# States' gate and val in seven products: one edit at the end of a recurrent-attention and SwiGLU kernel on one Trainium2 core

## The chip, the cores and the metric

The kernel runs on one core of a Trainium2 chip. TensorE (PE) multiplies, VectorE (DVE) and ScalarE (ACT) work element by element, GpSimd (POOL) does some more of that, and SyncE (SP) issues most of the DMA transfers. The engines run beside each other and wait for each other by semaphores; each takes its own instructions in the order in which the program lists them. The metric is the device time in microseconds; lower is better. All data are float32.

## The reference

Two stages follow each other. The first is a cross attention between 512 tokens and 32 states for each of 8 batches and 8 heads of width 64. The second is a SwiGLU feed-forward layer on all 8 x (512 + 32) = 4352 rows.

```python
# attention, per batch and head: x is (512, 64), state is (32, 64)
xread = softmax(scale * x @ state.T) @ state      # 512 rows: the tokens
sread = softmax(scale * state @ x.T) @ x          # 32 rows: the states
rows  = concatenate([xread, sread])               # heads side by side: 512 columns

# feed-forward, d_model = 512, d_ff = 1536
xn  = rows / sqrt(mean(rows**2) + 1e-6) * rms_g
g   = xn @ w_gate
val = xn @ w_val
out = (g * sigmoid(g) * val) @ w_out
```

What the change touches is `g`, `val` and the output of the 8 x 32 = 256 state rows.

## The kernel before

**Seven products.** A product of two matrices, each cut into 2 x 2 blocks, takes eight products of blocks. By the Strassen-Winograd scheme it takes seven, at the price of sums and differences of blocks. The kernel uses it for the output of every row but batch 0's (`project_seven`) and for gate and val of the tokens of batches 1 to 7 (`hidden_seven`). In `hidden_seven` a pair of hidden blocks (`mp`, six pairs of 2 x 128 columns) is one round: seven products, accumulated in the PSUM banks x, y and z, copied by ScalarE (`copies`, L570), added by VectorE (`sums`, L584). Bank x is written four times in a round: after its first and second product ScalarE copies it, after its third VectorE adds it to `c22`, and after that the round's last product is accumulated on top. Between the third and the last stand the first two products of the next pair.

**Stages.** Up to about 126 us the weights are brought into their form and batch 0 is computed. Then one period of about 98 us follows for each of batches 1 to 7: gate, val and output of one batch's tokens, and between them the attention of the next batch. After batch 7 comes the stretch of the states, which this case is about.

**The states before.** All 256 state rows are held transposed in `xsT` (4 parts of 128 model columns x 256 rows). For each of the 12 hidden blocks, `hidden` (L475) computes gate and val by plain products, 4 calls each over the 4 parts, with weights from `w_m` (L832). Here the stationary operand is a 128 x 128 block of weights and the moving operand has 256 columns. ScalarE applies Silu (L492), VectorE multiplies (L496), and for the upper six blocks it forms the sums that the output needs (L501, L503). Then `project_seven(NT, store_states)` gives the output, with the order of its steps written out in L839: p a product, c a copy by ScalarE, k a sum by VectorE. Each of its seven products is 6 calls (L677) of 256 columns. Its stores are cut into four pieces of 32 rows each, one DMA per piece, all on SyncE (L746).

**Order.** Inside `tc.manual_schedule` the order of TensorE, VectorE and ScalarE is dealt by hand: each letter of `ORDER` (up to batch 0) and `PERIOD` (each later batch) takes one step of the generator of that name. In the last period the stream `a` runs `state_norm` (L404): it squares `xsT` (L407), sums over the model columns (L412), takes the power -1/2 on GpSimd (L245), spreads the result over the rows by two transposes (L252) and scales `xsT` (L422). `paced` (L769) lets six letters pass after each of its steps. The stretch of the states stands behind the last period, with no order by hand.

**Weights in transit.** The weights of one pair, gate and val together, are one tile `w_m` of 1 MB, fetched from `w_d` by SyncE (`fetch`, L140) into one of three buffers. A buffer is fetched into again when TensorE has used it. When the stretch of the states begins, the tiles of pairs 0 to 2 are there; those of pairs 3 to 5 are fetched during it.

Of the kernel before, what the change touches and what calls it, by code (L numbers as in the profile page):

```python
# [17 lines left out]
P = 128  # L18
# [14 lines left out]
    "aaksacccassppakckpaaackasaapakapaskaaaswpksksswsxxwxxpxcspcskx"  # L33
)
# [3 lines left out]
def kernel(  # L38
# [365 lines left out]
    def state_norm():  # L404

        sq = one.tile([P, NI, NT], F32, name="sqT", tag="eS")
        SE.activation(out=sq, in_=xsT, func=ACTF.Square, scale=DM ** -0.5)  # L407
        yield
        sp = aps.tile([P, NT // P], F32, name="at")
        for r in range(NT // P):  # L410
            for i in range(NI):
                TE.matmul(out=sp[:, r:r + 1], lhsT=sq[:, i, P * r:P * r + P], rhs=ones,  # L412
                          start=(i == 0), stop=(i == NI - 1))
# [61 lines left out]
    def hidden(m, n, lhs, rhs, banks):  # L475


        gp, vp = [], []
        t = []
        h = hb[:, m, :]  # L480

        def products():
            for k, to in enumerate((gp, vp)):
                to.append(banks[k].tile([P, S], F32, name="pv" if banks[k] is vps else "f"))
                for i, r in enumerate(rhs):
                    TE.matmul(out=to[0][:, 0:n], lhsT=lhs(i, k), rhs=r,  # L486
                              start=(i == 0), stop=(i == len(rhs) - 1))
                yield

        def silu():  # L490
            t.append(two.tile([P, S], F32, name="t", tag="g"))
            SE.activation(out=t[0][:, 0:n], in_=gp[0][:, 0:n], func=ACTF.Silu)  # L492
            yield

        def gated():
            VE.tensor_tensor(out=h[:, 0:n], in0=t[0][:, 0:n], in1=vp[0][:, 0:n], op=ALU.mult)  # L496
            if "s" in seven and m >= HM:

                k = m - HM
                upper, lower = hb[:, k, 0:n // 2], hb[:, k, n // 2:n]  # L500
                VE.tensor_tensor(out=seven["s"][:, k, 0:n // 2], in0=lower, in1=hb[:, m, n // 2:n],  # L501
                                 op=ALU.add)
                VE.tensor_tensor(out=lower, in0=upper, in1=lower, op=ALU.subtract)  # L503
            yield

        return products(), silu(), gated()


# [11 lines left out]
    def hidden_seven(b):  # L520


        pairs = [{} for mp in range(NM // 2)]

        def product(ps, lhs, rhs, start):
            for i in range(2):
                TE.matmul(out=ps[:, i, :], lhsT=lhs[:, i, :], rhs=rhs, start=(start and i == 0),  # L527
                          stop=True, skip_group_check=True)

        def products():  # L530
            tt = aT_t[b]
            b11, t3, b21, b22 = (aT_s[b][:, e, HS * i:HS * i + HS]
                                 for e in range(2) for i in range(2))

            def first(mp, q):
                v, _ = v_sb[b, mp]
                a11, q["a12"], q["s3"], q["a22"] = (v[:, e, :, k, :]
                                                    for k in range(2) for e in range(2))
# [4 lines left out]
                _, vs = v_sb.pop((b, mp))  # L543
                q["vs"] = vs
                product(q["z"], vs[:, 0], tt[:, 0], True)
                yield

            def last(q):
                product(q["x"], q["a22"], tt[:, 2], False)

            yield from first(0, pairs[0])
            for mp, q in enumerate(pairs):
                if mp:
                    last(pairs[mp - 1])
                    yield
                product(q["x"], q["vs"][:, 1], tt[:, 1], False)
                yield
                product(q["z"], q["vs"][:, 2], b22, False)
# [9 lines left out]
            yield  # L568

        def copies():  # L570
            for mp, q in enumerate(pairs):
                g = q["g"] = two.tile([P, 2, 2, HS], F32, name="g", tag="g")
                SE.copy(g[:, :, 0, :], q["x"])
                yield
                q["c"] = seven["c22"].tile([P, 2, HS], F32, name="c22")
                SE.copy(q["c"], q["z"])
                yield
                SE.copy(g[:, :, 1, :], q["x"])  # L578
                yield
                SE.activation(out=hb[:, 2 * mp:2 * mp + 2, :], func=ACTF.Tanh, scale=0.5,  # L580
                              in_=g.rearrange("p m c t -> p m (c t)"))
                yield

        def sums():  # L584
            for mp, q in enumerate(pairs):
                h = hb[:, 2 * mp:2 * mp + 2, :]
                g = q["g"]
                for to, ps in ((g[:, :, 1, :], "z"), (g[:, :, 0, :], "y"), (q["c"], "x")):
                    VE.tensor_tensor(out=to, in0=to, in1=q[ps], op=ALU.add)  # L589
                    yield  # L590
                VE.scalar_tensor_tensor(out=h, in0=h, scalar=1.0, op0=ALU.add, op1=ALU.mult,  # L591
                                        in1=g.rearrange("p m c t -> p m (c t)"))
                yield
                for i, val in ((1, q["c"]), (0, q["x"])):
                    half = h[:, :, HS * i:HS * i + HS]
                    VE.scalar_tensor_tensor(out=half, in0=half, scalar=0.5, in1=val,
                                            op0=ALU.mult, op1=ALU.mult)
                    yield
                if 2 * mp >= HM:
                    k = 2 * mp - HM  # L600
                    upper, lower = (hb[:, k:k + 2, HS * i:HS * i + HS] for i in range(2))
                    VE.tensor_tensor(out=seven["s"][:, k:k + 2, :], in0=lower, in1=h[:, :, HS:S],
                                     op=ALU.add)
# [57 lines left out]
    def project_seven(n, store):  # L661
# [7 lines left out]
        def product(name, lhs, rhs):  # L669
# [5 lines left out]
            for r in range(R):  # L675
                for k in range(HM):
# [28 lines left out]
        def copies():  # L705

            for what, name in (("p1", "x"), ("p5", "z"), ("u2", "x"), ("c21", "x")):
                for r in range(R):
                    to = kept[what, r] = pool.tile([P, HD], F32, name="ot2")
                    SE.copy(to, banks[name][:, r, :])  # L710
                    if what == "c21":
                        store(R + r, 0, HD, to)
# [30 lines left out]
    def store_states(r, c0, n, ot):  # L743
        for j in range(4):
            r0 = T * (4 * r + j) + S
            nc.sync.dma_start(out=out[r0:r0 + Ns, c0:c0 + n], in_=ot[Ns * j:Ns * j + Ns, :])  # L746
# [3 lines left out]
    def of_batch_0(part):  # L750

        for m in range(NM):
            if m not in parts_0:
                parts_0[m] = hidden(m, S, lambda e, k, m=m: v_sb[0, m // 2][0][:, e, m % 2, k, :],
                                    [aT_s[0][:, e, :] for e in range(2)], (vps, vps))
# [50 lines left out]
    for b in range(1, B):  # L806
# [3 lines left out]
        h, t, u = hidden_seven(b)  # L810
# [10 lines left out]
        else:  # L821
            others = paced(state_norm())
# [48 lines left out]
```

## Time and profile before

| | us |
|---|---|
| median of 3 runs (806.21 to 806.81) | 806.23 |
| the profiled execution | 806.07 |
| its span, first to last instruction | 804.3 |
| from the states' gate and val to their output (742.17 to 781.02) | 38.85 |
| the states' output (781.02 to 800.05) | 19.03 |
| the tail behind the last matmul | 4.25 |

The page cuts the span into 40 slices and shows the busy tenths of each engine in them:

```profile
PE   4599999999999999999999999999999999999997
PEld 2243444788778887888778877888788877888886
DVE  4999996588347842786368834784278626841121
ACT  4888864553245323543255324532354325401110
POOL 0000003530154005500443025400550044200000
PEclk9699999999999999999999999999999999999999
```

Each digit is a fortieth of the span, some 20 us. PEld is TensorE's loading of stationary operands, which can lie beside its matmuls. The periods are seen as a pattern of about five digits in DVE, ACT and POOL; in the last three digits (from about 744 us) these engines have little to do. PEclk is the clock granted to TensorE, in tenths of full speed.

A row of the tables below names the line, the engine, the operation, what is written from what, the shape, the count, the busy time in us, the mean in ns of one, and the idle time before it. In a timeline the first column is the start and the second the time from there to the end of the last instruction of that row.

### The profile page before, as it was taken

Reading aid. Unit: us, or ns where it says so; the run is one execution under the profiler, and the core shown is the slowest. Engines: PE = TensorE matmul, PEld = TensorE weight load, DVE = VectorE, ACT = ScalarE, POOL = GpSimd, SP = SyncE. Lnnn points to the kernel's source line nnn. Section 1 sums busy time; section 2 is a strip of 40 time slices with the busy share of each in tenths; the row PEclk is TensorE's granted clock in tenths of the full one; section 3 lists DMA queues with packets and bytes.
Section 4 is the critical chain, followed back from the end, with each engine's and each line's share of the span. In section 5 each row is a group of like instructions: output and inputs, shape, how many; then the busy total and the mean of one; then the engine's idle time right before and its main releaser. Section 6 shows DMA issues by size and latency. Waiting matters only on the chain.

```text
span 804.3 us, 11772 instructions
## 1 busy us (share of the span) xinstructions
PE 779.2 (97%) x4678; PEld 592.5 (74%) x4678; DVE 493.3 (61%) x746; ACT 341.1 (42%) x560; POOL 178.4 (22%) x215
## 2 busy tenths in 40 slices
PE   4599999999999999999999999999999999999997
PEld 2243444788778887888778877888788877888886
DVE  4999996588347842786368834784278626841121
ACT  4888864553245323543255324532354325401110
POOL 0000003530154005500443025400550044200000
PEclk9699999999999999999999999999999999999999
DMA  9788745600172007300460017200630035001401
GB/s 294 229 287 298 262 160 185 259 31 13 36 269 105 1 24 248 152 1 18 150 241 17 14 44 261 106 1 20 233 115 2 13 145 208 2 14 38 147 12 27
DMA packets 61591, 94.09 MB, mean 117 GB/s; under 512 B 38752, under 2 KB 46432, under 8 KB 54624
## 3 DMA queue, kind: packets, MB, share of 16 engines
q1 hardware_dynamic: 59456, 92.81, 33.4%
q8 instruction: 37, 0.61, 0.3%
q10 hardware_dynamic: 2080, 0.52, 0.3%
q14 instruction: 18, 0.15, 0.1%
HBM read 78.12 MB, written 15.20 MB: 116 GB/s over the span
## 4 chain that ended last, share of the span: by engine, by line
PE 94%; DVE 4%; issue 0%; ACT 0%; DMA 0%; SPq 0%; DVEq 0%
PE f L677 35%; PE f L527 32%; PE f L486 5%; PE f L617 5%; PE pv L486 4%; PE at L444 3%; PE pv L444 3%; PE at L273 2%; PE at L282 1%; PE at L327 1%; PE at L341 1%; PE at L388 1%; DVE ex L223 1%; PE at L376 1%; DVE raw L219 1%; PE at L252 1%
## 5 line engine op out<-in xcount | busy, mean ns | idle before, releaser
L677 PE MATMUL f<-wo,hb 128*128 128x256 f32 x540 | 124.1, 382 | 0.6 <-ACT ot L710 0.5
L527 PE MATMUL f<-aT_s,v 128*128 128x256 f32 x504 | 119.6, 381 | 0.0
L677 PEld LDWEIGHTS f<-wo,hb 128*128 128x128 f32 x540 | 101.4, 190 | 20.5 <-ACT ot L710 7.3
L527 PEld LDWEIGHTS f<-aT_s,v 128*128 128x128 f32 x504 | 93.7, 190 | 17.3 <-issue 5.2
L589 DVE TENSOR_TENSOR g<-g,f 128x512 f32<-128x512 f32 x84 | 57.6, 687 | 78.2 <-PE f L527 74.9
L245 POOL TENSOR_TENSOR ri<-ss,mhalf 128x4 f32<-128x4 f32 x8 | 9.1, 1141 | 364.4 <-DVE ss L345 364.4
L527 PE MATMUL f<-aT_t,vs 128*128 128x256 f32 x336 | 87.1, 382 | 0.0
L677 PE MATMUL f<-wt,hs 128*128 128x256 f32 x360 | 80.3, 379 | 0.0
L677 PEld LDWEIGHTS f<-wt,hs 128*128 128x128 f32 x360 | 68.4, 190 | 9.3
L527 PEld LDWEIGHTS f<-aT_t,vs 128*128 128x128 f32 x336 | 62.6, 190 | 15.4 <-issue 6.2
L710 ACT COPY ot<-f 128x256 f32<-128x256 f32 x60 | 21.4, 371 | 121.6 <-PE f L677 121.6
L580 ACT ACTIVATE hb<-g 128x1024 f32<-128x1024 f32 x42 | 44.4, 1057 | 55.0 <-DVE g L589 55.0
L591 DVE SCALAR_TENSOR_TENSOR hb<-hb,g 128x1024 f32<-128x1024 f32 x42 | 55.4, 1320 | 8.0 <-ACT hb L580 8.0
L473 POOL TENSOR_TENSOR vs<-v,vs 128x256 f32<-128x256 f32 x42 | 58.3, 1388 | 0.0
L470 POOL TENSOR_TENSOR vs<-v 128x256 f32<-128x256 f32 x42 | 30.6, 728 | 118.5 <-ACT v L455 118.5
L578 ACT COPY g<-f 128x512 f32<-128x512 f32 x42 | 24.6, 586 | 67.4 <-PE f L527 67.4
L486 PE MATMUL pv<-aT_s,v 128*128 128x512 f32 x96 | 45.2, 611 | 1.1 <-DVE aT_s L351 1.1
L617 PE MATMUL f<-wo,hb 128*128 128x512 f32 x96 | 44.7, 600 | 0.0
L527 PE MATMUL f<-aT_t,v 128*128 128x256 f32 x168 | 43.9, 383 | 0.0
L527 PE MATMUL f<-aT_s,vs 128*128 128x256 f32 x168 | 43.1, 379 | 0.0
L677 PE MATMUL f<-wt,hb 128*128 128x256 f32 x180 | 42.5, 386 | 0.0
L486 PE MATMUL f<-xsT,w_m 128*128 128x256 f32 x192 | 42.1, 379 | 0.0
(116 smaller groups left out, 1213.7 us busy)
## 6 DMA issues: line engine op xcount, KB each, us to landing
w_m<-w_d SPq DMA_DIRECT2D x48, 1024.0 KB, 6.6
x_b<-in_x_dram SPq DMA_DIRECT2D x30, 256.0 KB, 4.0
out_dram<-ot SPq DMA_DIRECT2D x56, 128.0 KB, 1.8
raw<-in_moe_w_val_dram SPq DMA_DIRECT2D x6, 1024.0 KB, 5.2
raw<-in_moe_w_out_dram SPq DMA_DIRECT2D x6, 1024.0 KB, 7.1
w_d<-w_m SPq DMA_DIRECT2D x6, 1024.0 KB, 4.9
raw<-in_moe_w_gate_dram SPq DMA_DIRECT2D x5, 1024.0 KB, 5.7
raw<-in_moe_w_gate_dram SPq DMA_DIRECT2D x2, 512.0 KB, 4.9
```

What stands on the lines that cost most here:

```text
L444: TE.matmul(out=pv[e][Ns * j:Ns * j + Ns, :], lhsT=stT_g[b][D * e:D * e + D, j, :], rhs=w[D * e:D * e + D, j].rearrange("p m k f -> p (m k ...
L470: GE.tensor_tensor(out=vs[:, 0], in0=a21, in1=a22, op=ALU.add)
L473: GE.tensor_tensor(out=vs[:, 2], in0=a12, in1=vs[:, 1], op=ALU.subtract)
L486: TE.matmul(out=to[0][:, 0:n], lhsT=lhs(i, k), rhs=r, start=(i == 0), stop=(i == len(rhs) - 1))
L527: TE.matmul(out=ps[:, i, :], lhsT=lhs[:, i, :], rhs=rhs, start=(start and i == 0), stop=True, skip_group_check=True)
L578: SE.copy(g[:, :, 1, :], q["x"])
L580: SE.activation(out=hb[:, 2 * mp:2 * mp + 2, :], func=ACTF.Tanh, scale=0.5, in_=g.rearrange("p m c t -> p m (c t)"))
L589: VE.tensor_tensor(out=to, in0=to, in1=q[ps], op=ALU.add)
L591: VE.scalar_tensor_tensor(out=h, in0=h, scalar=1.0, op0=ALU.add, op1=ALU.mult, in1=g.rearrange("p m c t -> p m (c t)"))
L617: TE.matmul(out=banks[r], lhsT=hb[:, m, P * r:P * r + P], rhs=wo[:, m, :], start=(m == 0), stop=(m == NM - 1))
L677: TE.matmul(out=banks[name][:, r, :], lhsT=lhs(k)[:, P * r:P * r + P], rhs=rhs(k), start=(start and r == 0 and k == 0), stop=(k == HM - 1) ...
L710: SE.copy(to, banks[name][:, r, :])
```

## The change

1. **Gate and val of the states in seven products.** `hidden_seven` becomes general: weights, tokens, number of rows and the activation are arguments. For the states the four blocks of a pair's weights are the halves of the model columns times gate and val, and the blocks of `xsT` are the same halves times 128 rows. Each of the seven products of a pair is now 2 hidden blocks x 2 parts of the contraction, so 4 calls with 128 moving columns.
2. **The sums of blocks.** `sums_of_w` forms, on VectorE, four sums of 512 columns for each pair's weights, the last in place in `w_m`; pair 0's are a part of the last period's stream `a`, those of pairs 1 to 5 a stream `y` of their own. `sums_of_x` forms four differences of 256 columns at the end of `state_norm`.
3. **The order.** A string `STATES` deals the whole stretch: h products, t copies, u sums, y weight sums, p, c and k the output. `paced` lets three letters pass in place of six. The fetch of a pair's weights follows the last product of the pair that used the buffer. In the program's list some first steps of the stretch (pair 0's opening products, the weight sums of pairs 0 to 2) stand between the last steps of batch 7's output.
4. **The states' output.** Product y is cut in two halves of 3 calls each, the second behind x's second product.
5. **The last stores.** The four stores behind the last copy alternate between SyncE's and ScalarE's queue.

Shortened to its core:

```diff
+STATES = (
+    "hyyyyhthyytthhhuuhtuhththhytuuhuuhthuhhtthyuhyyutyhhhuuuttyuhhutyyhhthuhyhuhuttu"
+    "yhuhttyuhuhuuhuthhyuthythytuhuuhuhutuuhuuppcpkcpcpukkcpkpkpc"
 )
...
+        sums_of_x()
         yield
...
+    def sums_of_w(mps):
+
+        for mp in mps:
+            a11, a12, a21, a22 = blocks_of_w(mp)
+            s12 = seven["v"].tile([P, 2, HI, 2, P], F32, name="v")
+            s4 = seven["vs"].tile([P, 3, 2, P], F32, name="vs")[:, 0:HI]
+            w_sums[mp] = s12[:, 0], s12[:, 1], s4
+            VE.tensor_tensor(out=s12[:, 0], in0=a21, in1=a22, op=ALU.add)
+            yield
+            VE.tensor_tensor(out=s12[:, 1], in0=s12[:, 0], in1=a11, op=ALU.subtract)
+            yield
+            VE.tensor_tensor(out=s4, in0=a12, in1=s12[:, 1], op=ALU.subtract)
+            yield
+            VE.tensor_tensor(out=a21, in0=a11, in1=a21, op=ALU.subtract)
+            yield
...
+    def sums_of_x():
+
+        tt = seven["late"].tile([P, 3, HI, P], F32, name="x_t")
+        b11, b12, b21, b22 = blocks_of_x()
+        x_sums.extend(tt[:, i] for i in range(3))
+        for to, a, b in ((tt[:, 0], b12, b11), (tt[:, 1], b22, tt[:, 0]), (tt[:, 2], b21, tt[:, 1]),
+                         (b12, b22, b12)):
+            VE.tensor_tensor(out=to, in0=a, in1=b, op=ALU.subtract)
...
         def product(ps, lhs, rhs, start):
             for i in range(2):
-                TE.matmul(out=ps[:, i, :], lhsT=lhs[:, i, :], rhs=rhs, start=(start and i == 0),
-                          stop=True, skip_group_check=True)
+                for k, (l, r) in enumerate(zip(lhs, rhs)):
+                    TE.matmul(out=ps[:, i, 0:half], lhsT=l[:, i, :], rhs=r,
+                              start=(start and i == 0 and k == 0),
+                              stop=(k == len(lhs) - 1), skip_group_check=True)
...
-            yield from product("y", A(0, 1), B(1, 0))
+            parts = (range(HM),) if R > 1 else (range(HM // 2), range(HM // 2, HM))
+            yield from product("y", A(0, 1), B(1, 0), parts[0])
             yield from product("x", S_, TS(1))
+            for ks in parts[1:]:
+                yield from product("y", A(0, 1), B(1, 0), ks)
...
-    def store_states(r, c0, n, ot):
+    def store_states(r, c0, n, ot, *more):
         for j in range(4):
             r0 = T * (4 * r + j) + S
-            nc.sync.dma_start(out=out[r0:r0 + Ns, c0:c0 + n], in_=ot[Ns * j:Ns * j + Ns, :])
+            queue = (nc.sync, *more)[j % (1 + len(more))]
+            queue.dma_start(out=out[r0:r0 + Ns, c0:c0 + n], in_=ot[Ns * j:Ns * j + Ns, :])
...
-            yield from range(6)
+            yield from range(3)
...
-            others = paced(state_norm())
+            others = paced(step for part in (state_norm(), sums_of_w([0])) for step in part)
...
-    for m in range(NM):
-        n = B * (NM // 2) + m // 2
-        for part in hidden(m, NT, lambda i, k: w_sb[n][:, i, m % 2, k, :],
-                           [xsT[:, i, :] for i in range(NI)], ((fx, fx), (fy, fz))[m % 2]):
-            for _ in part:
-                pass
-        if m % 2:
-            fetch(n + W_BUFS)
-    p, c, k = project_seven(NT, store_states)
-    for step in (p, c, p, c, k, p, k, p, c, k, p, k, p, k, p, c):
-        next(step)
-
+    n = B * (NM // 2)
+    h, t, u = hidden_seven(NT, (state_weights, state_sums), state_tokens, True,
+                           lambda mp: fetch(n + mp + W_BUFS))
+    p, c, k = project_seven(NT, store_states, nc.scalar)
+    streams = {"h": h, "t": t, "u": u, "p": p, "c": c, "k": k, "y": sums_of_w(range(1, NM // 2))}
+    with tc.manual_schedule(**by_hand):
+        for stream in STATES:
+            next(streams[stream])
```

`blocks_of_w` and `blocks_of_x` return the four blocks of a pair's weights and of `xsT`; `state_weights`, `state_sums` and `state_tokens` hand them on, cut into the two parts of the contraction.

More of the change, by code (lines that the diff above doesn't have):

```diff
@@ L33 @@
     "aaksacccassppakckpaaackasaapakapaskaaaswpksksswsxxwxxpxcspcskx"
+)
+STATES = (
+    "hyyyyhthyytthhhuuhtuhththhytuuhuuhthuhhtthyuhyyutyhhhuuuttyuhhutyyhhthuhyhuhuttu"
+    "yhuhttyuhuhuuhuthhyuthythytuhuuhuhutuuhuuppcpkpcpukkcpkpkpc"
 )
@@ L473, in more_of_v, with hidden @@
         GE.tensor_tensor(out=vs[:, 2], in0=a12, in1=vs[:, 1], op=ALU.subtract)
-    def hidden(m, n, lhs, rhs, banks):
+    def hidden(m, lhs, rhs):
         gp, vp = [], []
@@ L483, in products @@
             for k, to in enumerate((gp, vp)):
-                to.append(banks[k].tile([P, S], F32, name="pv" if banks[k] is vps else "f"))
+                to.append(vps.tile([P, S], F32, name="pv"))
                 for i, r in enumerate(rhs):
-                    TE.matmul(out=to[0][:, 0:n], lhsT=lhs(i, k), rhs=r,
+                    TE.matmul(out=to[0], lhsT=lhs(i, k), rhs=r,
                               start=(i == 0), stop=(i == len(rhs) - 1))
@@ L491, in silu @@
             t.append(two.tile([P, S], F32, name="t", tag="g"))
-            SE.activation(out=t[0][:, 0:n], in_=gp[0][:, 0:n], func=ACTF.Silu)
+            SE.activation(out=t[0], in_=gp[0], func=ACTF.Silu)
             yield
         def gated():
[L496 to L503, printed above, removed]
+            VE.tensor_tensor(out=h, in0=t[0], in1=vp[0], op=ALU.mult)
             yield
@@ L518, in slot_sums, with weights_of, blocks, sums @@
         GE.tensor_tensor(out=b12, in0=b22, in1=b12, op=ALU.subtract)
-    def hidden_seven(b):
+    def weights_of(b):
+        def blocks(mp):
+            v, _ = v_sb[b, mp]
+            return [[v[:, e, :, k, :]] for k in range(2) for e in range(2)]
+        def sums(mp):
+            _, vs = v_sb.pop((b, mp))
+            return [[vs[:, i]] for i in range(3)]
+        return blocks, sums
+    def tokens_of(b):
+        return ([[aT_s[b][:, e, HS * i:HS * i + HS]] for e in range(2) for i in range(2)],
+                [[aT_t[b][:, i]] for i in range(3)])
@@ new lines, with blocks_of_w @@
+    w_sums = {}
+    x_sums = []
+    HI = NI // 2
+    def blocks_of_w(mp):
+        w = w_sb[B * (NM // 2) + mp]
+        return [w[:, HI * e:HI * e + HI, :, k, :] for k in range(2) for e in range(2)]
+    def sums_of_w(mps):
[12 more added lines that the diff above has]
+            yield
@@ new lines, in each, with state_weights, state_sums, blocks_of_x @@
+    def each(t):
+        return [t[:, i] for i in range(HI)]
+    def state_weights(mp):
+        return [each(t) for t in blocks_of_w(mp)]
+    def state_sums(mp):
+        return [each(t) for t in w_sums[mp]]
+    def blocks_of_x():
+        return [xsT[:, HI * e:HI * e + HI, P * i:P * i + P] for e in range(2) for i in range(2)]
+    def sums_of_x():
[5 more added lines that the diff above has]
+            VE.tensor_tensor(out=to, in0=a, in1=b, op=ALU.subtract)
@@ L523, in hidden_seven, with state_tokens @@
+    def state_tokens():
+        return [each(t) for t in blocks_of_x()], [each(t) for t in x_sums]
+    def hidden_seven(n, weights, tokens, silu, after=lambda mp: None):
         pairs = [{} for mp in range(NM // 2)]
+        half = n // 2
+        blocks, block_sums = weights
         def product(ps, lhs, rhs, start):
             for i in range(2):
-                TE.matmul(out=ps[:, i, :], lhsT=lhs[:, i, :], rhs=rhs, start=(start and i == 0),
-                          stop=True, skip_group_check=True)
+                for k, (l, r) in enumerate(zip(lhs, rhs)):
+                    TE.matmul(out=ps[:, i, 0:half], lhsT=l[:, i, :], rhs=r,
+                              start=(start and i == 0 and k == 0),
+                              stop=(k == len(lhs) - 1), skip_group_check=True)
@@ L530, in products @@
         def products():
-            tt = aT_t[b]
-            b11, t3, b21, b22 = (aT_s[b][:, e, HS * i:HS * i + HS]
-                                 for e in range(2) for i in range(2))
+            (b11, t3, b21, b22), tt = tokens()
             def first(mp, q):
-                v, _ = v_sb[b, mp]
-                a11, q["a12"], q["s3"], q["a22"] = (v[:, e, :, k, :]
-                                                    for k in range(2) for e in range(2))
+                a11, q["a12"], q["s3"], q["a22"] = blocks(mp)
@@ L542, in first @@
                 q["z"] = fz.tile([P, 2, HS], F32, name="f")
-                _, vs = v_sb.pop((b, mp))
-                q["vs"] = vs
-                product(q["z"], vs[:, 0], tt[:, 0], True)
+                q["s"] = block_sums(mp)
+                product(q["z"], q["s"][0], tt[0], True)
                 yield
             def last(q):
-                product(q["x"], q["a22"], tt[:, 2], False)
+                product(q["x"], q["a22"], tt[2], False)
             yield from first(0, pairs[0])
@@ L554, in products @@
                     last(pairs[mp - 1])
+                    after(mp - 1)
                     yield
-                product(q["x"], q["vs"][:, 1], tt[:, 1], False)
+                product(q["x"], q["s"][1], tt[1], False)
                 yield
-                product(q["z"], q["vs"][:, 2], b22, False)
+                product(q["z"], q["s"][2], b22, False)
                 yield
@@ L568, in products, with gates @@
             yield
+        def gates(q):
+            return [q["g"][:, :, i, 0:half] for i in range(2)]
         def copies():
             for mp, q in enumerate(pairs):
-                g = q["g"] = two.tile([P, 2, 2, HS], F32, name="g", tag="g")
-                SE.copy(g[:, :, 0, :], q["x"])
+                q["g"] = two.tile([P, 2, 2, HS], F32, name="g", tag="g")
+                SE.copy(gates(q)[0], q["x"][:, :, 0:half])
                 yield
-                q["c"] = seven["c22"].tile([P, 2, HS], F32, name="c22")
-                SE.copy(q["c"], q["z"])
+                q["c"] = seven["c22"].tile([P, 2, HS], F32, name="c22")[:, :, 0:half]
+                SE.copy(q["c"], q["z"][:, :, 0:half])
                 yield
-                SE.copy(g[:, :, 1, :], q["x"])
+                SE.copy(gates(q)[1], q["x"][:, :, 0:half])
                 yield
-                SE.activation(out=hb[:, 2 * mp:2 * mp + 2, :], func=ACTF.Tanh, scale=0.5,
-                              in_=g.rearrange("p m c t -> p m (c t)"))
+                SE.activation(out=hb[:, 2 * mp:2 * mp + 2, 0:n].rearrange("p m (c t) -> p m c t", c=2),
+                              in_=q["g"][:, :, :, 0:half], func=ACTF.Silu if silu else ACTF.Tanh,
+                              scale=1.0 if silu else 0.5)
                 yield
@@ L585, in sums @@
             for mp, q in enumerate(pairs):
[L586 to L589, printed above, removed]
+                h = hb[:, 2 * mp:2 * mp + 2, 0:n]
+                for to, ps in ((gates(q)[1], "z"), (gates(q)[0], "y"), (q["c"], "x")):
+                    VE.tensor_tensor(out=to, in0=to, in1=q[ps][:, :, 0:half], op=ALU.add)
                     yield
[L591 to L597, printed above, removed]
+                if not silu:
+                    VE.scalar_tensor_tensor(out=h, in0=h, scalar=1.0, op0=ALU.add, op1=ALU.mult,
+                                            in1=q["g"].rearrange("p m c t -> p m (c t)"))
+                    yield
+                for i, val in ((1, q["c"]), (0, q["x"][:, :, 0:half])):
+                    part = h[:, :, half * i:half * i + half]
+                    if silu:
+                        VE.tensor_tensor(out=part, in0=part, in1=val, op=ALU.mult)
+                    else:
+                        VE.scalar_tensor_tensor(out=part, in0=part, scalar=0.5, in1=val,
+                                                op0=ALU.mult, op1=ALU.mult)
                     yield
@@ L600, in sums @@
                     k = 2 * mp - HM
-                    upper, lower = (hb[:, k:k + 2, HS * i:HS * i + HS] for i in range(2))
-                    VE.tensor_tensor(out=seven["s"][:, k:k + 2, :], in0=lower, in1=h[:, :, HS:S],
-                                     op=ALU.add)
+                    upper, lower = (hb[:, k:k + 2, half * i:half * i + half] for i in range(2))
+                    VE.tensor_tensor(out=seven["s"][:, k:k + 2, 0:half], in0=lower,
+                                     in1=h[:, :, half:n], op=ALU.add)
                     yield
@@ L659, in weight_sums, with project_seven @@
                 yield
-    def project_seven(n, store):
+    def project_seven(n, store, *more):
         half = n // 2
@@ L667, in project_seven, with product @@
         banks = {}
-        def product(name, lhs, rhs):
+        def product(name, lhs, rhs, ks=range(HM)):
             start = name not in banks
@@ L675, in product @@
             for r in range(R):
-                for k in range(HM):
+                for k in ks:
                     TE.matmul(out=banks[name][:, r, :], lhsT=lhs(k)[:, P * r:P * r + P], rhs=rhs(k),
@@ L711, in copies @@
                     if what == "c21":
-                        store(R + r, 0, HD, to)
+                        store(R + r, 0, HD, to, *more)
                     yield
@@ L753, in of_batch_0 @@
             if m not in parts_0:
-                parts_0[m] = hidden(m, S, lambda e, k, m=m: v_sb[0, m // 2][0][:, e, m % 2, k, :],
-                                    [aT_s[0][:, e, :] for e in range(2)], (vps, vps))
+                parts_0[m] = hidden(m, lambda e, k, m=m: v_sb[0, m // 2][0][:, e, m % 2, k, :],
+                                    [aT_s[0][:, e, :] for e in range(2)])
             yield from parts_0[m][part]
@@ L809 @@
             load_x(b + 2)
-        h, t, u = hidden_seven(b)
+        h, t, u = hidden_seven(S, weights_of(b), lambda b=b: tokens_of(b), False)
         p, c, k = project_seven(S, store_tokens(b))
@@ L829 @@
         assert all(next(stream, done) is done for stream in streams.values() if stream is not others)
-    for m in range(NM):
-        n = B * (NM // 2) + m // 2
-        for part in hidden(m, NT, lambda i, k: w_sb[n][:, i, m % 2, k, :],
-                           [xsT[:, i, :] for i in range(NI)], ((fx, fx), (fy, fz))[m % 2]):
-            for _ in part:
-                pass
-        if m % 2:
-            fetch(n + W_BUFS)
-    p, c, k = project_seven(NT, store_states)
-    for step in (p, c, p, c, k, p, k, p, c, k, p, k, p, k, p, c):
-        next(step)
+    n = B * (NM // 2)
[6 more added lines that the diff above has]
+            next(streams[stream])
+    assert all(next(stream, done) is done for stream in streams.values())
 _INS = ['x', 'state', 'moe_w_gate', 'moe_w_val', 'moe_w_out', 'moe_rms_g']
```

## The prediction

> **What bounds the kernel now.** I read the page's busy shares first, then the chain of waits over the last 90 us, then the timeline at the few places that the change touches.
>
> ```profile
> PE 779.2 (97%) x4678; PEld 592.5 (74%) x4678; DVE 493.3 (61%) x746; ACT 341.1 (42%) x560; POOL 178.4 (22%) x215
> L486 PE MATMUL f<-xsT,w_m 128*128 128x256 f32 x192 | 42.1, 379 | 0.0
> ```
>
> TensorE is busy 97% of the span, so only TensorE time and the tail count. The row of the states' gate and val has 192 records for 96 calls (12 blocks, gate and val, 4 parts of the contraction): one fp32 call is two records, each with its own weight load.
>
> ```profile
> 742.33 38.85 PE f L486 x180
> 781.18 10.37 PE f L677 x48
> 791.55 0.02 issue
> 791.58 0.38 ACT ot L710
> 791.96 0.04 issue
> 792.00 8.05 PE f L677 x36
> 800.05 0.02 issue
> 800.08 0.37 ACT ot L710
> ```
>
> This is the chain of waits: start, duration, what. From 742 us to the end it is TensorE alone, except one copy at 791.58 and the last copy at 800.08. 180 records in 38.85 us are 215.8 ns each, so 192 are **41.4 us**. After the last copy nothing computes until 804.3.
>
> **Products: 192 records of 256 columns become 336 of 128.** Six pairs, seven products, 2 blocks, 2 parts of the contraction are 168 calls, 336 records. Columns streamed fall to 336x128 = 43,008 from 49,152, which is 7/8. But a record of 128 columns has half the matmul time to hide the same 128x128 weight load. No row shows an fp32 product of that shape; two are near.
>
> ```profile
> 168.64 0.60 PE L273 MATMUL at<-ident,x_b 128*128 128x128 f32 x4
> 168.97 0.52 PEld L527 LDWEIGHTS f<-aT_t,v 128*128 128x128 f32 x3
> ...
> 169.08 0.60 PE L527 MATMUL f<-aT_t,v 128*128 128x256 f32 x2
> ...
> 692.46 1.97 PEld L412 LDWEIGHTS at<-ones,sqT 128*128 128x128 f32 x16
> 692.67 1.84 PE L412 MATMUL at<-ones,sqT 128*128 128x1 f32 x16
> 694.35 0.30 PEld L527 LDWEIGHTS f<-aT_s,v 128*128 128x128 f32 x2
> ```
>
> (Timeline: start, duration.) Four transposes with 128 columns follow each other from 168.64 to 169.08: 110 ns each, loads of 128x128 hidden. Their loads are of a cheaper kind, though (mean 152 ns in the groups by shape, against 190 for the products'). The second row is the products' own load with almost nothing to hide under: 16 from 692.46 to 694.35, the first of which waited 216 ns behind a 256-column matmul; the other 15 take (1890-216)/15 = 112 ns. If loads and matmuls overlap as everywhere else in this trace, a 128-column record costs the larger of 110 and 112: 336 x 0.112 = **37.6 us, 3.8 less**. The bounds are 110 ns (36.9 us) and no overlap at all.
>
> Against this stands a rule. The Trainium skill, "TensorE: Matmul & The Clock Gate", section "Back-to-back issue gap", says that in a real stream of load and matmul pairs both set the spacing: about 81 ns at 128 columns, where the bare formula gives 55.8. Scaling our 110 by 81/55.8 (an estimate) gives 160 ns, 336 x 0.160 = 53.8 us: **12.4 us more** than before. I take the rows: at 256 columns this trace shows 215.8 ns, which is no more than twice the 110 of the transposes, so the load adds nothing there, and the load alone sustains 112.
>
> **Stalls that come.** The order in which the changed program lists its instructions gives two.
> - Batch 7's projection shares bank x with ScalarE's copies, and the states' first products are put between to cover them.
>
> ```profile
> 727.49 1.03 PE L486 MATMUL f<-xsT,w_m 128*128 128x256 f32 x4
> 727.69 0.37 ACT L710 COPY ot<-f 128x256 f32<-128x256 f32 x1 [3.08 <-PE f L677]
> ```
>
> The copy is over at 728.06, 0.57 us after TensorE left the bank, some 0.61 with the signal. Four records of 0.216 (0.86 us) covered it. The first pair's opening product is now dealt as 3 calls at the first copy, 1 call here: 2 x 0.112 = 0.22 us, so TensorE waits **0.39**. The other covers are 3 calls, 0.67 us, and hold.
> - The last pair has no next pair behind it: its seventh product follows the sixth directly on bank x, and VectorE must add bank x to c22 between. From the end of a matmul to the start of its reader are 0.20 us (727.49 to 727.69), the add of 256 columns 0.42 (row L496), the signal 0.04: **0.66**. At the other pairs two products of the next pair, 1.8 us, stand between.
>
> **Stalls that go.** At 791.55 TensorE waits for ScalarE's copy of bank x; the timeline gives 0.46 us of idle before L677 there. Now half of product y (6 records, 1.29 us) stands after x's second product: **0.46 less**. The other half must cover the subtraction L725, which starts 0.20 after product z and takes 0.96: about 1.20 with the signal, against 1.29. Late next is that subtraction, with 0.1 to spare.
>
> **What must stay hidden.**
> - VectorE, weight sums: four of 512 columns a pair, 0.69 each (row L602), 16.6 us in all. Ten of the 24 are listed before that stretch, where VectorE idles; the remaining 14 (9.7 us), with 36 operations of 256 columns at 0.42 (15 us), make 25 us beside 37.6 of TensorE.
> - VectorE at 705 us: xsT's scaling (1.6 us) and the four new differences (4 x 0.42) now stand before the last pair's gating, which used 0.40 of waiting. hs ended at 707.2 and comes about 2.9 later, 710.1; the fifth call of L677 wt,hs wants it at 708.27+1.73, and 0.2 later because the two transposes of L252 now come earlier: 710.2. Bounds 0 and 0.6; I take 0, since the sum ends just inside.
> - The norm's chain: L252 moves from 713.24 to 697.7 on TensorE. GpSimd's power (1.14) is then fed at 694.5 and done at 695.8: 2 us to spare. Uncovered, TensorE would stand for that remainder.
> - Weight fetches (SyncE): the first waits for pair 0's last product at 747.5 and lands 4.6 later (the fetch of 746.7 landed at 751.3); pair 3 wants its blocks at 758.4. Behind it on SyncE stand only later fetches and the last stores. VectorE's weight sums of pair 3 stand behind that landing; they are due at 753, where it has just landed.
> - ScalarE: the table load for Silu (1.28) falls between copies with 1.5 us before the next is due.
>
> **The last stores.**
>
> ```profile
> x_b<-in_x_dram ACTq DMA_DIRECT2D x2, 256.0 KB, 3.4
> ...
> L746 SPq DMA_DIRECT2D out_dram<-ot x16: 314/419/423, 789.5 to 801.8; - x16
> ...
> DMA to landing us min/median/max: 1.5/1.6/1.6
> ```
>
> The last copy ends at 800.45; the fourth store behind it starts at 801.8. With two per queue the last starts one issue (0.42) after the first, 800.87: **0.93 less**. ScalarE's queue is used only at the start in this trace, with landings no longer than SyncE's (3.4 against 4.0 for the same 256 KB), so I take the full gain. Nothing excludes a loss from a queue idle for 800 us: if it landed after 3.4 in place of 1.6, 1.8-0.93 = 0.9 would be lost. These are the bounds.
>
> **Sum.** -3.8 (products) -0.46 -0.93 +0.39 +0.66 = -4.1. The profiled execution took 806.07 (span 804.3 and 1.8 around it), so 801.9; it lies 0.16 under the median of 806.23, which gives **802.1**.
>
> **Rivals.**
> 1. *The load does not hide (slower).* If each matmul waits for its whole load of 190 ns, 336 x 0.190 = 63.8: +22.4 -0.3 = 828. By the skill's rule 818. It decides from a pitch of 124 ns: (41.4+0.3)/336. For it: the untried shape, and loads of 190. Against: 15 loads at 112.
> 2. *VectorE comes late in the stretch.* It works in order, and each pair's adds now share it with weight sums that wait for transfers. One add late by 0.66 at each of five pair boundaries costs 3.3: 805.4, within no change. Against: 25 us of work in 37.6.
> 3. *Better than summed.* 110 ns, and the 0.39 filled: 0.7+0.39 less, 801.0.
> 4. *The second queue brings nothing:* 803.0, or 803.9 at its worst bound.
>
> **Chances.** Forecast 0.66 (801.3 to 803.0), rival 3 0.12, rival 4 0.06, rival 2 0.10, rival 1 0.06. The range 800.3 to 804.4 holds the first three and the small end of rival 2. Within 0.2% (804.6 to 807.8; runs of this kernel can't be told apart more finely) lies half of rival 2: faster 0.89, same 0.05, slower 0.06.
>
> **What would show it.** Right: a product row of 336 records starting 112 ns apart; the stretch from 742 to the projection near 36.5 us; idle TensorE of 0.4 near 727 and 0.7 just before the projection, none at its second x product; the last store starting 0.4 after the last copy. Wrong: a pitch above 124, or idle TensorE at each pair released by VectorE.

## The result, and the profile after

| | before | after | difference |
|---|---|---|---|
| median | 806.26 | 802.39 | -3.87 |
| lowest to highest of 4 runs | 806.21 to 806.81 | 801.79 to 804.07 | |
| the profiled execution | 806.07 | 802.44 | -3.63 |
| its span | 804.3 | 800.7 | -3.6 |

The ratio of after to before is 0.9954, with a 95% interval of 0.9937 to 0.9971. Forecast were 802.1 and a range of 800.3 to 804.4. In a later session the changed kernel took 802.01 (801.85 to 803.61) beside 806.61 (805.87 to 807.44) for the kernel before, a ratio of 0.9949 [0.9935, 0.9962].

The first fence is the page after: engines, busy us, share of the span, instructions; then DVE's busy tenths in 40 slices.

```profile
PE 775.7 (97%) x4822; PEld 594.2 (74%) x4822; DVE 515.1 (64%) x786; ACT 347.0 (43%) x572; POOL 178.0 (22%) x215
DVE  5989997588337852786358833785178735891461
```

TensorE has 144 more matmul records and 3.5 us less busy time. VectorE's slice from about 704 to 724 us shows 9 tenths in place of 4, and the two from about 744 to 783 us show 4 and 6 in place of 1 and 2; but for the two waits told below, TensorE does not pay for it. The next fence is the chain of waits over the stretch of the states (start, duration, what).

```profile
724.37 0.67 PE f L596 x6
725.04 2.67 PE f L750 x12
727.70 0.02 issue
727.73 0.38 ACT ot L787
728.11 0.04 issue
728.15 10.63 PE f L750 x48
738.78 0.67 PE f L596 x6
739.45 2.65 PE f L750 x12
742.10 35.08 PE f L596 x314
777.17 0.02 issue
777.19 0.43 DVE c L658
777.63 0.04 issue
777.67 1.16 PE f L596 x8
778.83 18.23 PE f L750 x84
797.06 0.02 issue
797.08 0.37 ACT ot L787
```

314 records in 35.08 us are 112 ns each. TensorE waits twice, for ScalarE's copy at 727.7 and for VectorE's add to `c22` at 777.2, at the two places that the forecast named. The states' output is now one piece of 84 records, with no copy in its middle. VectorE's weight sums and the weight fetches appear nowhere in the chain.

### The profile page after: what moved, and what is told of

Read it like the earlier page. It is cut to its first block, busy times and chain, and to the rows that moved or that the text cites. A ratio compares the mean times of both kernels' runs of the same rounds, so it can differ in the third digit from the quotient of the medians.

```text
span 800.7 us, 12112 instructions
## 1 busy us (share of the span) xinstructions
PE 775.7 (97%) x4822; PEld 594.2 (74%) x4822; DVE 515.1 (64%) x786; ACT 347.0 (43%) x572; POOL 178.0 (22%) x215
## 4 chain that ended last, share of the span: by engine, by line
PE 94%; DVE 4%; ACT 1%; issue 0%; DMA 0%; SPq 0%; DVEq 0%
PE f L596 37%; PE f L750 35%; PE f L690 5%; PE pv L492 4%; PE at L450 3%; PE pv L450 3%; PE at L278 2%; PE at L332 1%; PE at L287 1%; PE at L346 1%; PE at L393 1%; PE at L381 1%; DVE ex L228 1%; DVE raw L224 1%; PE at L257 1%; DVE w_m L233 0%
## 5 line engine op out<-in xcount | busy, mean ns | idle before, releaser
L658 DVE TENSOR_TENSOR g<-g,f 128x512 f32<-128x512 f32 (+1 forms) x96 | 62.8, 654 | 90.0 <-PE f L596 86.6
L649 ACT ACTIVATE hb<-g 128x1024 f32<-128x1024 f32 (+1 forms) x48 | 48.2, 1004 | 63.0 <-DVE g L658 63.0
L647 ACT COPY g<-f 128x512 f32<-128x512 f32 (+1 forms) x48 | 26.9, 561 | 76.7 <-PE f L596 76.7
L750 PE MATMUL f<-wo,hs 128*128 128x256 f32 x180 | 41.6, 382 | 0.0
```

What stands on the lines that cost most here:

```text
L647: SE.copy(gates(q)[1], q["x"][:, :, 0:half])
L649: SE.activation(out=hb[:, 2 * mp:2 * mp + 2, 0:n].rearrange("p m (c t) -> p m c t", c=2), in_=q["g"][:, :, :, 0:half], func=ACTF.Silu if s ...
L658: VE.tensor_tensor(out=to, in0=to, in1=q[ps][:, :, 0:half], op=ALU.add)
L750: TE.matmul(out=banks[name][:, r, :], lhsT=lhs(k)[:, P * r:P * r + P], rhs=rhs(k), start=(start and r == 0 and k == 0), stop=(k == HM - 1) ...
```

## The experiments

Three stretches of each trace are compared. The first is the **early part**, up to the last period's score products (L282 before, L287 after). The second is the **late part**, from there to the start of the last matmul. The third is the **tail**, from the end of the last copy to the end of the span. The early part is the same program in all kernels, but ends at 613.4 to 615.2 us. This scatter arises in its first 65 to 67 us, while weights are loaded and converted: from the second set of score products, which starts there, to its end the early part takes 548.1 us in every kernel. So parts of the change are read from the late part and the tail, which repeat within 0.02 us between two profiled runs of the changed kernel.

| kernel | early ends | late part | tail |
|---|---|---|---|
| before | 613.62 | 186.04 | 3.84 |
| changed | 613.95 | 182.72 | 3.21 |
| changed, profiled once more | 613.87 | 182.72 | 3.21 |
| last stores on one queue | 615.16 | 182.71 | 3.84 |
| product y whole | 614.29 | 183.35 | 3.21 |
| 64 moving columns | 613.70 | 182.63 | 3.19 |
| only y in halves and two queues | 614.29 | 185.40 | 3.18 |
| paced by six letters | 613.91 | 182.88 | 3.21 |
| last add covered | 613.41 | 181.94 | 3.21 |
| last add covered, second run | 613.55 | 181.94 | 3.22 |
| both covered, copies of bank x moved | 614.82 | 182.49 | 3.21 |
| the same, one store of 128 rows | 614.56 | 182.50 | 6.06 |
| both covered | 613.91 | 181.49 | 3.21 |

**Last stores on one queue.** This undoes the fifth part alone.

```diff
-    p, c, k = project_seven(NT, store_states, nc.scalar)
+    p, c, k = project_seven(NT, store_states)
```

> The four last stores all on SyncE again, all else as in the changed kernel. If the second queue saves what the issues behind the last copy take, the fourth store starts 1.3 us after the copy (0.45 with two queues) and the time from the last copy's end to the end of the span grows from 3.2 to 3.8 us: +0.6, as the two traces differ, rather than the 0.93 of the prediction. If ScalarE's queue brings nothing (rival 4), that stretch stays within 0.2 of 3.2.

The tail is 3.84, as before the change, and the late part is the same within 0.01. The second queue is worth **0.63**. Rival 4 falls. The whole time of this one run (804.27) says little, since its early part was 1.2 us longer.

**Product y whole.** This undoes the fourth part alone. One letter p goes from the string. (In the diff ahead of the prediction the end of `STATES` has a letter c too many: it ends in `uuppcpkpcpukkcpkpkpc`.)

```diff
-            parts = (range(HM),) if R > 1 else (range(HM // 2), range(HM // 2, HM))
+            parts = (range(HM),)
```

> Product y of the states' output whole again, before x's second product. By the sum TensorE stands idle about 0.46 us before x's third product, released by ScalarE's copy of bank x, and the states' output takes 18.2 + 0.46 = 18.7 us. If the halves only moved the wait, the output stays at 18.2.

The fence is the timeline of this kernel at x's third product; the bracket gives the idle time before a row and what ended it.

```profile
786.77 2.75 PE L750 MATMUL f<-wt,hs 128*128 128x256 f32 x12
...
789.56 0.37 ACT L787 COPY ot<-f 128x256 f32<-128x256 f32 x1 [4.81 <-PE f L750]
...
789.99 2.21 PE L750 MATMUL f<-wo,hb 128*128 128x256 f32 x9 [0.46 <-ACT ot L787]
```

The wait is back, with 0.46 in the bracket, but the late part is longer by **0.63**. The starts of the rows show more of it. The 12 records of the first row start 216 ns apart, so they occupy 786.77 to 789.36, and the next could have started at 789.36; it starts at 789.99, some **0.62** later. The bracket counts from the end of the last matmul (789.52). A matmul of 256 columns is shown 379 ns long, while the next starts 216 ns after it: the bracket leaves out the difference of 0.16.

Two smaller terms, read from the starts of single records in the traces, nearly cancel. Behind the wait, the second record comes 320 ns after the first in place of 216, which is 0.10 more: the row of 9 records takes 2.21, and 9 such records that waited for nothing (at 784.83 in this trace) take 2.11. Against that, the halves have a small wait of their own in the changed kernel, in front of x's second product:

```profile
784.05 0.96 DVE L802 TENSOR_TENSOR hs<-hs,hb 128x768 f32<-128x768 f32 x1 [4.42 <-PE f L750]
785.12 2.46 PEld L750 LDWEIGHTS f<-wt,hs 128*128 128x128 f32 x12 [0.22 <-issue]
785.15 2.83 PE L750 MATMUL f<-wt,hs 128*128 128x256 f32 x12
```

The subtraction ends at 785.01. What it writes is the weights of this product, so the first load, which without a wait starts some 0.2 ahead of its matmul, comes late too. The product starts 0.01 late, and its 12 records take 2.83 in place of 2.75: 0.09 in all. So the wait that went cost 0.73, and 0.09 came back.

**64 moving columns.** The matmuls, copies, adds and activations of the states' gate and val take 64 of every 128 columns. Half of the state rows' gate and val is left out; the weight loads are the same.

```diff
+        cols = half // 2 if silu else half
...
-                    TE.matmul(out=ps[:, i, 0:half], lhsT=l[:, i, :], rhs=r,
+                    TE.matmul(out=ps[:, i, 0:cols], lhsT=l[:, i, :], rhs=r[:, 0:cols],
```

> Each product of the states' gate and val streams 64 columns in place of 128; the copies, sums and activations of that stretch take half the columns too, so half of the state rows' gate and val is left out. The weight loads are unchanged. If the load sets the pitch (112 ns, as in the row of 16 loads), the records stay 112 ns apart and the stretch from 742 to the output stays near 36.9 us. If the 128 columns set it (110 ns, as the transposes), the pitch falls well under 100 ns, towards 55, and the stretch falls under 30 us.

This is the chain of waits of this kernel, its longest piece of gate and val:

```profile
742.17 34.80 PE f L597 x312
```

34.80 us for 312 records are again 112 ns. Half of the columns, and the pitch (the time from one record's start to the next one's) stays: the **weight load sets the pitch**, and 64 columns cost what 128 cost. The timelines show how it looks: first the changed kernel, then this one, one load row and one matmul row each.

```profile
743.83 2.76 PEld L596 LDWEIGHTS f<-xsT,w_m 128*128 128x128 f32 x24
743.94 2.84 PE L596 MATMUL f<-xsT,w_m 128*128 128x128 f32 x24
```

```profile
743.68 2.76 PEld L597 LDWEIGHTS f<-xsT,w_m 128*128 128x128 f32 x24
743.74 2.84 PE L597 MATMUL f<-xsT,w_m 128*128 128x64 f32 x24
```

24 loads take 2.76 us in both; the mean of one load, 190 to 192 ns, is longer than their distance, because two loads overlap. The matmuls themselves are not what takes 112 ns: at 742.01 us in the second trace, behind a product of 256 columns under which the first load was already done, two matmuls of 64 columns start 56 ns apart. Loads of another size were not tried, so what in a load takes the 112 ns stays open.

**Only y in halves and two queues.** The kernel before with the fourth and fifth part, and plain products for gate and val. `product` takes `ks`, and the order of the output's steps becomes:

```diff
-    for step in (p, c, p, c, k, p, k, p, c, k, p, k, p, k, p, c):
+    for step in (p, c, p, c, k, p, p, c, p, k, k, p, k, p, k, p, c):
```

> The kernel before with only the last two parts of the change: product y in halves and the last stores on two queues; gate and val stay plain products of 256 columns. By the sum, as corrected by the two traces: the output takes 19.03 - 0.46 = 18.6 us, the tail 0.6 less, together -1.1; the stretch of gate and val stays at 38.85. What is left of the change, about -2.6, would then be the seven products with their two new stalls. If the seven products brought nothing (rival 2), this kernel would be as fast as the changed one.

The late part is 0.64 shorter than before and the tail 0.66 shorter, -1.30 together, not -1.1: the removed stall again counts for 0.64 (0.73 less 0.09; the small wait before x's second product is in this trace too). The rest of the late part, 185.40 - 182.72 = **2.68**, is what the seven products bring with their two stalls. Rival 2, under which they would bring nothing, falls.

**Last add covered.** The output's first product is dealt between the last pair's sixth and seventh product.

```diff
-    "yhuhttyuhuhuuhuthhyuthythytuhuuhuhutuuhuuppcpkpcpukkcpkpkpc"
+    "yhuhttyuhuhuuhuthhyuthythytuhuuhuhutuuphuupcpkpcpukkcpkpkpc"
```

> The first product of the states' output is dealt between the last pair's sixth and seventh product, so 1.3 us of TensorE work and more stand over VectorE's add of bank x. By the sum TensorE's 0.68 us there disappear, the output begins 0.7 earlier, and nothing else becomes late: the last pair's hs is then due 1.7 us after its product and takes about 1.1. If the wait only moves (to the fifth call of product z), the gain is smaller than 0.3.

Chain of waits of this kernel, at the end of gate and val:

```profile
741.56 35.06 PE f L596 x314
776.62 2.59 PE f L750 x12
779.21 0.89 PE f L596 x8
780.10 15.64 PE f L750 x72
```

The output's first product (776.62) now covers the add, the last pair's seventh product (779.21) finds bank x free, and no VectorE step is left in the chain. The late part is **0.78** shorter: 0.68 of wait, and 0.10 behind it. In the changed kernel the seventh product's loads begin only when the wait is over (777.67), and its second record comes 213 ns after the first in place of 112; here it comes 109 ns after. Nothing came back later. It was then timed in one session with the changed kernel:

> The changed kernel with the last pair's add covered by the output's first product, timed: 0.7 to 0.8 us less than the changed kernel in the same session, 181.9 from the last period's score products to the last matmul.

> The changed kernel once more, beside the two above. From the last period's score products to the last matmul 182.7, as before within 0.1; the whole time between 801.8 and 804.1, since what differs from run to run lies in the first 65 us.

In that session it took 801.34 (801.13 to 802.10) and the changed kernel 802.01. The late parts came out at 181.94 and 182.72, as expected. The whole times differ by 0.67, with ranges that overlap; the late part is the evidence.

**Paced by six letters.** `paced` as before the change; all weight sums in the stream y, for which four letters y are put in front of `STATES`.

```diff
-            yield from range(3)
+            yield from range(6)
...
-            others = paced(step for part in (state_norm(), sums_of_w([0])) for step in part)
+            others = paced(state_norm())
```

> paced lets six letters pass again, and all the weight sums, pair 0's too, are in the stream y. The norm's two transposes and the scaling of xsT go back to about 714 us and the differences of xsT to 718, which are wanted by TensorE from 724. If the prediction's reading is right that there is room on both sides, the time from the last period to the last matmul changes by less than 0.3 us. If moving the norm forward was needed, TensorE stands before the states' first products.

The late part is 182.88, 0.16 longer, and the stretch of the states has no wait more. The 0.16 stands near 691 us: in this trace, as in that of the kernel before, two records there start 305 and 291 ns after the one ahead of them in place of 216, and in the changed kernel they do not. So moving the norm forward was not needed to feed the states' products; it gained 0.16 at another place, which the sum did not have.

**Both covered.** The other stall, at 727.7, comes from a cover that is too short. Product y of pair 0 was dealt second, so that there is more to put under the copy.

```diff
-            yield from first(0, pairs[0])
+            def cross(q):
+                q["y"] = fy.tile([P, 2, HS], F32, name="f")
+                product(q["y"], q["a12"], b21, True)
+
+            opening = first(0, pairs[0])
+            yield next(opening)
+            if silu:
+                cross(pairs[0])
+                yield
+            yield from opening
...
-                q["y"] = fy.tile([P, 2, HS], F32, name="f")
-                product(q["y"], q["a12"], b21, True)
-                yield
+                if mp or not silu:
+                    cross(q)
+                    yield
```

> The changed kernel with both new stalls covered: product y of pair 0 is dealt second, so that three calls stand at ScalarE's copy at 727 in place of one, and the output's first product covers the last pair's add. By the sum 0.41 + 0.68 = 1.1 us less TensorE time than the changed kernel and no idle TensorE over 0.1 us from 700 us on; about 801.3 where the changed kernel takes 802.4. If a covered wait comes back elsewhere, less.

In this first form the letters were left as they were, so that each of the next steps of h came one letter later and ScalarE's second copy of bank x stood before pair 0's second product; pair 0's gate is therefore another. The late part fell by 0.23 only. A timeline of this kernel shows the missing time:

```profile
743.94 0.38 ACT L656 COPY g<-f 128x256 f32<-128x256 f32 x1
...
744.37 1.16 PE L596 MATMUL f<-x_t,v 128*128 128x128 f32 x8 [0.74 <-ACT g L656]
```

The second product, which writes bank x, had to wait for that copy. With one letter moved (`hyyyyhthyytthhh` became `hyyyyhhthyytthh`) the copy stands where it was in the changed kernel:

> Both new stalls covered, with the stream's letters in an order in which bank x's copies keep their places (ScalarE's second copy of bank x after the second product, as in the changed kernel). By the sum 1.1 us less than the changed kernel from the last period to the last matmul (182.7 there from the period's score products, so 181.6), no idle TensorE over 0.1 us from 700 us on, and about 801.3 where the changed kernel takes 802.4. The 0.74 of waiting at 744 in the run with both covers must be gone; if it stays, the cover at 727 is paid back there.

Chain of waits of this kernel, whole from 724 us on:

```profile
724.33 0.67 PE f L596 x6
725.00 2.65 PE f L759 x12
727.65 0.67 PE f L596 x6
728.32 10.42 PE f L759 x48
738.74 0.67 PE f L596 x6
739.40 2.65 PE f L759 x12
742.06 34.61 PE f L596 x310
776.67 2.59 PE f L759 x12
779.26 0.89 PE f L596 x8
780.15 15.64 PE f L759 x72
795.80 0.02 issue
795.82 0.37 ACT ot L796
```

Six records under each copy, and TensorE alone up to the last copy. The late part is 181.49, **1.23** under the changed kernel's. The median, 801.35 us (800.90 to 802.28), is below that of both kernels; the ratio to before is 0.9938 [0.9925, 0.9950]. The second cover, 0.45 of it, does not show in the whole time (801.34 without it, 801.35 with it), because the early part scatters by more; only the trace shows it.

**One store of 128 rows.** The first form with both covers, and in it the four stores behind each result as one, the last as two of 64 rows on two queues.

```diff
+        rows_ = out.rearrange("(b t) f -> b t f", t=T)[4 * r:4 * r + 4, S:T, c0:c0 + n]
+        if more:
+            nc.sync.dma_start(out=rows_[0:2], in_=ot[0:2 * Ns, :])
+            more[0].dma_start(out=rows_[2:4], in_=ot[2 * Ns:4 * Ns, :])
```

> As the kernel with both stalls covered; in addition the four stores of 32 rows behind each result of the states become one of 128 rows, the last one two of 64 rows, one on each queue. The last store is then issued right behind the last copy and not 0.45 us later: 0.4 us less tail if a store of 64 rows lands as fast as one of 32, nothing if it lands that much later.

The tail grew from 3.21 to **6.06**, and the whole time to 804.97 from 803.09. A miss. The windows of this kernel behind the last copy (granted clock, DMA share and GB/s stand last):

```profile
799.00:800.00 1.00, 0.00 (x0) 0.00 (x0) 0.00 (x0) 0.00 (x0) 0.00 (x0) 1.00 0.12 27
800.00:801.00 1.00, 0.00 (x0) 0.00 (x0) 0.00 (x0) 0.00 (x0) 0.00 (x0) 1.00 0.13 32
801.00:802.00 1.00, 0.00 (x0) 0.00 (x0) 0.00 (x0) 0.00 (x0) 0.00 (x0) 1.00 0.13 47
```

With the stores of 32 rows (the same kernel otherwise) one microsecond holds most of the work:

```profile
799.00:800.00 1.00, 0.00 (x0) 0.00 (x0) 0.00 (x0) 0.00 (x0) 0.00 (x0) 1.00 0.48 123
```

A share of 0.13 of 16 DMA engines is what two engines make that are always busy, and it stays there for three microseconds. The Trainium skill, "DMA: Bandwidth & Descriptors", section "Why a DMA increments its semaphore by 16 and not by 1", says that the number of engines is the largest up to 16 that divides the sizes of both sides' slowest dimension. Here the destination's is 2 blocks, which gives two; for 32 rows it is 16. The row agrees with it; which engines worked is not in the profile, and other shapes were not compared. The issue of ScalarE's store also took 1.37 us in this trace, where one of 32 rows takes 0.38 to 0.43, and how the 2.85 divides between the two was not tried.

## Why the prediction was right, point by point

| term of the sum | forecast | measured | from |
|---|---|---|---|
| 336 records of 128 columns in place of 192 of 256 | -3.8 | -3.9 | pitches: 336 x 111.7 ns, 192 x 215.8 ns |
| wait before x's third product removed | -0.46 | -0.64 | y whole (0.63); only y in halves |
| last stores on two queues | -0.93 | -0.63 | one queue |
| new wait at 727 | +0.39 | +0.51 | starts of records; 0.45 of it goes in both covered |
| new wait before the last product | +0.66 | +0.78 | last add covered |
| norm moved forward, not in the sum | 0 | -0.16 | paced by six letters |
| the two other covers of 3 calls, taken to hold | 0 | +0.12 | starts of records |
| early part, not in the sum | 0 | +0.33 | run to run |
| sum | -4.1 | -3.6 | spans |

- **Products.** The row of 16 loads was the right one: 112 ns forecast, 112 measured, and the 64 columns show that it is the load. Rival 1 falls, and with it the estimate of 160 ns: no such pitch was seen. The bound of 110, and with it rival 3's first half, was not reached: in the long pieces of every chain the products' loads stand 112 ns apart.
- **The stall that went** was mis-sized by 0.18. Two steps failed. The first was "the timeline gives 0.46 us of idle", read off the bracket; the starts of the rows give 0.62, and 0.10 more was lost behind the wait. The second was the subtraction "with 0.1 to spare", which was counted up to the product's matmul, where its weight load starts earlier: 0.09 came back there.
- **The new stalls** were worked out from starts, and the waits were right within 0.02 (0.40 and 0.68). Each lost 0.10 more behind it, which the sum did not have.
- **The other covers** "are 3 calls, 0.67 us, and hold": they were short by 0.06 each. In the kernel with both covers ScalarE's copy ends at 724.74, and the next product's first load starts at 724.79; at the loads' pitch it would have started at 724.72.
- **One step behind these small terms.** The prediction counted each cover up to the next product's matmul. The traces show that a wait stops that product's first weight load, which otherwise starts 0.1 to 0.2 ahead of the matmul. This is read from the starts; no run was made to try it.
- **The last stores** were mis-sized by 0.30. The store that landed last was issued 0.45 us behind the copy in place of 1.31, so 0.87 was saved at the issue; the 0.93 came from a start rounded to 801.8 (it is 801.76). And it was one of ScalarE's queue, whose landing took 1.7 us in place of 1.6, and the kernel's closing waits took 1.03 in place of 0.97 after it. This is a comparison of two traces; why ScalarE's store lands later was not tried.
- **What had to stay hidden** stayed hidden. VectorE's differences of `xsT` delayed the last pair's `hs` to 709.95 (forecast 710.1); the first weight fetch of the stretch was issued at 748.6 (forecast 747.5), with no wait for it. Rival 2's late adds were not seen at any of the five pair boundaries.
- **The early part** added 0.33 in the profiled run. Without it the span would have fallen by 3.95 (3.32 in the late part and 0.63 in the tail), against the 4.14 of the sum. That the two are so close is in part luck: the stores, the new stalls and the other covers gave some 0.66 less than forecast, and the stall that went, the products and the norm some 0.44 more. Its scatter is the reason why single times of these kernels can't tell such parts apart.

## What to carry to other kernels

When a product is cut so that its moving side becomes short, look for a row that has the same weight load with less to hide under it: its pitch, not the length of a load, is the floor. Count a stall by the starts of the instructions around it, not by the idle time before the second; add the 0.10 that the records behind it lost in these traces; and let a cover reach up to the next product's weight load, not only to its matmul. Give each wait of a shared bank its cover in calls times pitch: 0.22 us under a copy that needs 0.61 is a stall that can be written down beforehand. A scheme with a next round under each wait has none under its last; borrow from the stage that follows.

## What the runs showed that was not expected

- A float32 product of 128 x 128 weights costs 112 ns per record at 64 and at 128 moving columns. At 256 it costs 216.
- Behind a wait for which the weight load waits too, the second record came 0.10 late: 320 ns in place of 216, and 213 in place of 112.
- Two stores of 64 rows, as two blocks of 32 each, made the tail 2.85 us longer than four stores of 32 rows, at a DMA share of 0.13.
- ScalarE issued its two stores in 0.38 and 0.43 us, like SyncE, after having issued none since the start of the kernel.
